# A transformer-like block: the second piece's product with v in float16 parts, earlier weight conversions, and products of ones on TensorE

## The chip, the core and the metric

One core of a Trainium2 chip runs the whole program. The metric is device time in microseconds of that core, as the median of several runs. TensorE multiplies matrices into PSUM; VectorE (DVE), ScalarE (ACT) and GpSimd (POOL) work on the results; SyncE (SP) issues nearly all transfers.

## What is computed

Attention over 2 batches, 8 heads, 768 positions and a head size of 64, with a window of 128 keys and 4 sink keys; then a layer norm and a two-layer channel network (512 to 2048 to 512) with a residual; then a gate by sine and cosine, a mixing over positions and a last channel product.

```python
scores = scale * np.matmul(q, k.transpose(0, 1, 3, 2))
scores = np.where(is_sink | in_window, scores, -1e9)
a = softmax(scores);  x = np.matmul(a, v)              # attention
xn = (x - mu) / np.sqrt(var + 1e-06) * g_ln
x = x + np.maximum(xn @ w_ch1, 0.0) @ w_ch2            # channel network
theta = x @ w_theta
y = einsum(w_tok_r, x * cos(theta)) + einsum(w_tok_i, x * sin(theta))
u = x + y
out = u + np.maximum(u @ w_ch, 0.0)
```

## The kernel before

The 1536 rows are cut into six pieces of two tiles of 128 rows. For each piece the attention runs head by head (`attn_fast`, a generator whose steps are drawn by the main loop): scores `s` (line 273), then the masked maximum on VectorE (394) and the exponential on ScalarE (397) into `p`. The channel network runs in 56 units `u`; a piece takes part in 16 of them (piece 0 in units 0 to 15, piece 1 in 8 to 23, and so on). In unit u, `first(u+1)` (649 or 670) computes one block of hidden values `h` and `second(u)` (696) adds its product to `acc`. The steps of the attention of the next piece are put between these parts by `advance`, so that TensorE's order is written out by hand; the queues of the other engines are ordered by a scheduler that goes by its own estimate of times. Each engine works its queue strictly in order.

Pieces 0 and 1 (`TURNED = 2`) turn their weights on TensorE: `turn_w` transposes `p` into a bank `wp` (443), and one engine, ScalarE for even heads (449) and VectorE for odd ones (447), copies it to `wt` in float32. One head later, `values` multiplies `wt` by `v` in float32 (477); each float32 product is two instructions in the trace. Sinks have their own small transpose (457), copy (458) and product. The result, divided by the sums, goes to `x` (494). For these pieces v is loaded whole (`whole_v`, 203). Pieces 2 to 5 split weights and v into a large and a small float16 part (`send_w`, `split_v` with lines 196 and 198), turn them by a transposing transfer (430), and need three float16 products for each float32 one.

Weights of the channel network come as 64-bit words. `load_w12(f)` reads two of 512 KB into raw buffers, of which there are four, and converts each with VectorE (555), ScalarE (556 and 558) and VectorE again (559). Four loads (`PRE`) are placed in piece 0's attention; later ones stand in the loop over units, held behind `relu` of that unit (`behind`). `AHEAD = (2, 3)` says that up to f = u + 2 is loaded in unit u, and up to u + 3 from unit 7 on. Units 0 to 7 use the weights in float32; from f = 8 they are split into two float32r parts first (637, 638).

The banks for `wp` are `ab[1:]` (three) during piece 0 and one, `a3`, later; `pv` has one bank during piece 1. `range_v` and `range_whole` find the largest v for a check at the end; `range_whole` loads tiles of v that were never split once more.

Of the kernel before, what the change touches and what calls it, by code (L numbers as in the profile page):

```python
# [8 lines left out]
F32 = mybir.dt.float32  # L9
F32R = mybir.dt.float32r  # L10
F16 = mybir.dt.float16
# [38 lines left out]
READY2 = 13.0  # L50
RATE = 7.0
PRE = [10, 15, 20, 24]
AHEAD = (2, 3)
START = 2
EARLY = 38.0

# [13 lines left out]
class Net:  # L70
# [110 lines left out]
    def split_v(self, b, t):  # L181

        if (b, t) in self.v3:
            return
        nc, p = self.nc, self.att
        r = p["vr"].tile([128, DM], F32, tag="vr", name="vr")
        nc.sync.dma_start(out=r, in_=self.vt[b, t])
        if t == NT:
            o = p["v"].tile([128, DM], F16, tag="vk", name="vk", bufs=1)
            nc.scalar.activation(o, r, AF.Copy, scale=VSC)  # L190
            r, lo, hi = r[64:96], o[64:96], o[64:96]
            self.v3[b, t] = o
        else:
            o = p["v"].tile([128, 2, DM], F16, tag="v", name="v")
            hi, lo = o[:, 0], o[:, 1]
            nc.scalar.activation(hi, r, AF.Copy, scale=VSC)
            self.v3[b, t] = hi, lo
        nc.vector.scalar_tensor_tensor(out=lo, in0=r, scalar=VSC, in1=hi, op0=ALU.mult, op1=ALU.subtract)
# [76 lines left out]
    def attn_fast(self, eng):  # L275

        steps = [(piece, h) for piece in range(NP) for h in range(H)]
        nc, p, qk, scored, turned, sent, late = self.nc, self.att, {}, [], [], [], []

        def load(j, eng=eng):  # L280
            if j < len(steps):
                piece, h = steps[j]
                if h % 2 == 0:
                    qk[piece, h] = qk[piece, h + 1] = self.split_qk(piece, h // 2, eng)

        def load_v(piece):
            if piece < NP:
                b, tiles = self.tiles(piece)
                if piece < TURNED:
                    for t in tiles:  # L290
                        self.whole_v(b, t)
                    return
                for t in ([tiles[0] - 1] if tiles[0] else []) + tiles + ([NT] if tiles[-1] >= 2 else []):
                    self.split_v(b, t)

        def ahead(piece):
            return self.tc.high_priority() if piece < TURNED else ExitStack()

        def turn():

            piece, h, pt, st = scored.pop(0)
            b, tiles = self.tiles(piece)
            with ahead(piece):
                blocks = self.turn_w(pt, tiles, h)
            sinks = []
            if tiles[0]:
                p["ws"].append(p["ws"].pop(0))
                sinks = [p["ws"][-1][0:NSK, i] for i in range(PIECE)]
                if not turned:

                    pool, tag = self.vbanks[self.vturn % len(self.vbanks)]
                    self.vturn += 1
                    with ahead(piece):
                        self.turn_sinks(pool.tile([128, 512], F32, tag=tag, name="pv"), pt, sinks)
            turned.append((piece, h, blocks, sinks, st, pt))

        def finish(head):

            piece, h, blocks, sinks, st = head[:5]
            b, tiles = self.tiles(piece)  # L320
            with ahead(piece):
                self.values(b, h, tiles, piece, blocks, sinks, st, turned[0] if turned and turned[0][3] else None)
                if h % (H // 2) == H // 2 - 1:
                    self.stats(piece, h // (H // 2))
            if h == V_RANGE:
                while late:
                    q, ts = self.tiles(late.pop())
                    for t in ts:
                        if (q, t) in self.v3:
                            with self.behind():  # L330
                                self.range_v(q, t)
            if h == H - 1:
                with ahead(piece):
                    self.norm(piece)
                late.append(piece)

        load(0, self.nc.vector)
        load_v(0)
        for j, (piece, h) in enumerate(steps):
            b, tiles = self.tiles(piece)  # L340
            if h == 0:
                self.x[piece] = self.xp.tile([128, PIECE, DM], F32, tag=f"x{piece}", name=f"x{piece}")
            load(j + 2)
            if h == (3 if piece else V_NEXT) and piece != TURNED - 1:
                load_v(piece + 1)
            pt, st = yield from self.softmax(h, tiles, qk[piece, h])
            if piece < TURNED:
                scored.append((piece, h, pt, st))
            else:
                sent.append((piece, h) + self.send_w(pt, tiles) + (st,))  # L350
            if piece < TURNED and h == H - 1:

                while scored:
                    turn()
                    yield
                    finish(turned.pop(0))
                    yield
                while turned:
                    finish(turned.pop(0))
                if piece == TURNED - 1:  # L360
                    load_v(piece + 1)
                yield
                continue
            if len(scored) > (TURN if piece < TURNED else 0):
                turn()
                yield

            if len(turned) > (1 if scored else 0):
                finish(turned.pop(0))
            elif len(sent) > LAG:  # L370
                finish(sent.pop(0))
        while sent:
            yield
            finish(sent.pop(0))
        for t in tiles:
            self.range_v(b, t)
        self.range_whole()

    def softmax(self, h, tiles, qk):

        nc, p = self.nc, self.att
        n = len(tiles)
# [2 lines left out]
        for i, t in enumerate(tiles):  # L385
# [10 lines left out]
                op1=ALU.min, accum_out=st[:, 0, i:i + 1]),  # L396
                nc.scalar.activation(e, e, AF.Exp, bias=st[:, 0, i:i + 1], scale=-1.0,  # L397
                                     accum_out=st[:, 1, i:i + 1])]
        self.inverse(st, PSC * VSC if qk[1] is not None else 1.0)
        return pt, st  # L400

    def send_w(self, pt, tiles):
# [30 lines left out]
    def turn_w(self, pt, tiles, h):  # L433

        nc = self.nc
        pool, tag = self.wbanks[self.wturn % len(self.wbanks)]
        self.wturn += 1
        ps = pool.tile([128, 512], F32, tag=tag, name="wp")
        keys = [(i, t - 1 + c) for i, t in enumerate(tiles) for c in range(2) if t + c]
        m = len(keys)  # L440
        for x, (i, t) in enumerate(keys):
            c0 = (t + 1 - tiles[i]) * KW
            nc.tensor.transpose(ps[:, x * 128:(x + 1) * 128], pt[:, i, c0:c0 + 128], self.ident)  # L443
        wt = self.att["wt"].tile([128, m, 128], F32, tag="wt", name="wt")
        ps = ps[:, 0:m * 128].rearrange("p (m k) -> p m k", k=128)
        if h % 2:
            nc.vector.tensor_copy(wt, ps)
        else:
            nc.scalar.activation(wt, ps, AF.Copy)
        return {(i, 0, t): wt[:, x] for x, (i, t) in enumerate(keys)}  # L450

    def turn_sinks(self, bank, pt, sinks):

        nc = self.nc
        ps = bank[0:NSK, 256:512].rearrange("p (i k) -> p i k", k=128)
        for i in range(PIECE):
            nc.tensor.transpose(ps[:, i], pt[:, i, 128:128 + NSK], self.ident)
        nc.vector.tensor_copy(self.att["ws"][-1][0:NSK], ps)

    def values(self, b, h, tiles, piece, blocks, sinks, st, after):  # L460

# [3 lines left out]
        pv = pool.tile([128, 512], F32, tag=tag, name="pv")  # L465
        hc = slice(h * D, (h + 1) * D)
        for i in range(len(tiles)):
            if piece < TURNED:
                prods = [(a, self.whole[b, t][:, hc]) for (j, e, t), a in blocks.items() if j == i]
                if sinks:  # L470
                    prods.append((sinks[i], self.whole[b, 0][0:NSK, hc]))
            else:
                prods = [(a, v[:, hc]) for (j, e, t), a in blocks.items() if j == i for v in self.v3[b, t][:2 - e]]
                if sinks:
                    prods.append((sinks[i], self.v3[b, NT][:, hc]))
            for j, (a, m) in enumerate(prods):
                nc.tensor.matmul(pv[:, i * D:(i + 1) * D], a, m, start=j == 0, stop=j == len(prods) - 1)  # L477
# [342 lines left out]
    def run(self, general):  # L820
# [27 lines left out]
        else:  # L848
# [2 lines left out]
            a["wbuf"] = [w.tile([128, 5 * PIECE, 128], F16, name=f"w{i}") for i in range(3)]  # L851
            for w in a["wbuf"]:
                nc.gpsimd.memset(w[:, 0:PIECE], 0.0)
            ws = rp("a_ws")
            a["ws"] = [ws.tile([128, PIECE, 128], F32, name=f"ws{i}") for i in range(2)]
            raw = rp("a_raw")
            attn = self.attn_fast
        self.rawp = [(self.xp, f"x{NP - 2 + i}") for i in range(2)] + ([] if general else [(raw, f"r{i}") for i in range(2)])
# [3 lines left out]
        pe = tc.manual_schedule(engines={mybir.EngineType.PE})  # L862
        pe.__enter__()
        side = attn(nc.vector)
        self.sbanks, self.vbanks, self.wbanks = [sb, hb, hb], [vb, ab[0]], ab[1:]
        self.tbanks = [hb, hb]
        n = 0
        while 0 not in self.xnorm:
            next(side)
            n += 1  # L870
            if n == 1:
                self.late()
            if n in PRE and not general:
# [225 lines left out]
```

## Time and profile before

| What | Value |
|---|---|
| runs | 617.91, 623.66, 625.28 us (median 623.66) |
| profiled execution | 617.65 us, of which the profile's span is 615.9 |
| busy, share of the span | TensorE 95%, VectorE 66%, ScalarE 54%, GpSimd 10% |
| mean granted TensorE clock | 0.983 |

All rows are of the one profiled execution, with times from the start of the span. TensorE's matrix products and its loading of weights are separate rows (PE and PEld). The end of a product is modelled, and products overlap, so that the time from one start to the next says more than the duration of one. Names such as `pv<-v,wt` are output and inputs; L477 is line 477. The granted clock is 1.00 at 2.4 GHz and half that at 1.2. In a row by stretch stand: start and end, length, then for PE, PEld, DVE, ACT and POOL the busy time with the number of instructions, the granted clock, the busy share of the transfer engines, and GB/s.

### The profile page before, as it was taken

To read this page: it belongs to the slowest core of one execution; us is meant where nothing else is said; L and a number is where in the kernel's file an instruction comes from. 1 tells how busy PE (TensorE), PEld (TensorE's weight loads), DVE (VectorE), ACT (ScalarE), POOL (GpSimd) and SP (SyncE) were. 2 spreads that over 40 slices of the span, in tenths; PEclk is the share of its full clock that TensorE was granted. 3 is DMA by queue.
4 is the path that set the end of the run, shared out by engine and by line. 5 is a ranking of instruction groups with operands and counts; after the bars stand their busy time and mean duration, and the time that the engine had idled before them with its cause. 6 is when DMAs were issued, how large, how long until landed. Compare 5 with 4: busy or idle time off the path is not lost.

```text
span 615.9 us, 9332 instructions
## 1 busy us (share of the span) xinstructions
PE 584.7 (95%) x3473; PEld 479.8 (78%) x3473; DVE 408.5 (66%) x925; ACT 334.0 (54%) x732; POOL 60.1 (10%) x53
## 2 busy tenths in 40 slices
PE   5969998899999999999999899999999899999996
PEld 3756666577777777777788678888999789999996
DVE  4763465889867776976775643367798789754262
ACT  3834563998755656655556633346676656532020
POOL 1000000000000000000021200001343332300100
PEclk9999997899999999999999989999999999999998
DMA  7641442789722533433312310000232322010112
GB/s 274 215 159 44 160 156 86 251 209 222 130 54 49 117 82 71 96 69 60 78 54 101 103 51 2 0 1 1 102 104 104 103 69 70 1 35 34 36 36 74
DMA packets 55367, 56.41 MB, mean 92 GB/s; under 512 B 40080, under 2 KB 43152, under 8 KB 55312
## 3 DMA queue, kind: packets, MB, share of 16 engines
q1 hardware_dynamic: 55312, 55.72, 32.0%
q8 instruction: 29, 0.48, 0.3%
q14 instruction: 26, 0.21, 0.1%
HBM read 43.12 MB, written 3.15 MB: 75 GB/s over the span
## 4 chain that ended last, share of the span: by engine, by line
PE 69%; DVE 13%; DMA 7%; ACT 6%; issue 2%; POOL 1%; SPq 0%; ACTq 0%; POOLq 0%
PE acc L696 19%; PE h L670 18%; PE s L273 9%; PE m L781 5%; PE f L812 5%; PE pv L477 5%; PE h L649 3%; DVE st L559 2%; DMA raw<-wtok 2%; DMA raw<-w 2%; PE th L740 2%; PE wp L443 2%; ACT st L558 1%; ACT raw L556 1%; DVE st L555 1%
## 5 line engine op out<-in xcount | busy, mean ns | idle before, releaser
L638 DVE TENSOR_TENSOR wl<-w,wh 128x512 fp32r<-128x512 f32 x96 | 69.0, 723 | 53.4 <-ACT wh L637 26.7
L637 ACT ACTIVATE wh<-w 128x512 fp32r<-128x512 f32 x96 | 59.9, 628 | 77.5 <-PE acc L696 44.0
L670 PE MATMUL h<-xT,wh 128*128 128x512 f32 (+1 forms) x384 | 96.8, 388 | 2.4 <-DVE w L555 2.4
L670 PEld LDWEIGHTS h<-xT,wh 128*128 128x128 f32 x384 | 67.1, 191 | 18.2 <-ACT xT L625 2.6
L696 PE MATMUL acc<-wh,hh 128*128 128x512 f32 x176 | 73.2, 416 | 0.0
L397 ACT ACTIVATE p<-p,st 128x272 f32<-128x272 f32 (+1 forms) x96 | 47.4, 494 | 43.7 <-DVE st L394 43.3
L696 PE MATMUL acc<-wl,hh 128*128 128x512 f32 x176 | 69.6, 395 | 0.0
L696 PE MATMUL acc<-wh,hl 128*128 128x512 f32 x176 | 69.5, 395 | 0.0
L394 DVE CUSTOM_DVE_ANT_0 p<-s,mask 128x272 f32<-128x272 f32 (+1 forms) x96 | 39.3, 411 | 29.7 <-PE s L273 28.9
L670 PE MATMUL h<-xT,wl 128*128 128x512 f32 (+1 forms) x192 | 48.8, 376 | 0.0
L696 PEld LDWEIGHTS acc<-wh,hh 128*128 128x128 f32 x176 | 33.5, 190 | 9.4 <-issue 1.2
L556 ACT ACTIVATE raw<-raw 128x512 f32<-128x512 f32 (+1 forms) x52 | 37.0, 715 | 6.5 <-DVE st L555 6.4
L670 PEld LDWEIGHTS h<-xT,wl 128*128 128x128 f32 x192 | 35.0, 191 | 6.8
L477 PE MATMUL pv<-v,wt 128*128 128x64 f16 (+1 forms) x472 | 38.2, 228 | 1.9 <-DVE x L494 1.9
L696 PEld LDWEIGHTS acc<-wh,hl 128*128 128x128 f32 x176 | 33.5, 190 | 7.8 <-DVE hl L675 0.3
L696 PEld LDWEIGHTS acc<-wl,hh 128*128 128x128 f32 x176 | 33.4, 190 | 6.0 <-DVE wl L638 0.4
L767 POOL TENSOR_TENSOR x<-xh,xl 128x512 f32<-128x512 f32 x12 | 19.3, 1607 | 131.1 <-DVE r L761 131.1
L597 POOL TENSOR_TENSOR rs<-rs,mhalf 128x2 f32<-128x2 f32 x6 | 4.8, 805 | 266.9 <-ACT rs L596 266.9
L675 DVE SCALAR_TENSOR_TENSOR hl<-h,hh 128x512 fp32r<-128x512 f32 (+1 forms) x48 | 30.7, 639 | 0.2 <-ACT hh L674 0.2
L273 PE MATMUL s<-raw 64*128 64x272 f32 (+1 forms) x64 | 24.1, 520 | 6.9 <-DMA raw<-qk 6.4
L558 ACT ACTIVATE st<-raw 128x768 uint16<-128x768 uint16 (+1 forms) x20 | 19.4, 971 | 18.6 <-DMA raw<-wtok 7.2
L674 ACT ACTIVATE hh<-h 128x512 fp32r<-128x512 f32 (+1 forms) x48 | 26.5, 552 | 5.5 <-PE h L670 5.5
(287 smaller groups left out, 1442.3 us busy)
## 6 DMA issues: line engine op xcount, KB each, us to landing
raw<-w SPq DMA_DIRECT2D x32, 512.0 KB, 4.3
raw<-wtok SPq DMA_DIRECT2D x12, 768.0 KB, 4.2
raw<-qk SPq DMA_DIRECT2D x16, 336.0 KB, 3.0
vr<-vt SPq DMA_DIRECT2D x14, 256.0 KB, 3.0
out_dram<-o SPq DMA_DIRECT2D x24, 128.0 KB, 1.7
raw<-qk SPq DMA_DIRECT2D x8, 272.0 KB, 4.0
raw<-wth SPq DMA_DIRECT2D x4, 512.0 KB, 3.3
raw<-wch SPq DMA_DIRECT2D x4, 512.0 KB, 3.3
```

Of the source, the lines that this page charges most:

```text
L273: self.nc.tensor.matmul(ps, q[:, c], k[:, k0:k0 + kn], start=j == 0, stop=j == len(prods) - 1)
L394: self.newest = [nc.vector.tensor_tensor_reduce(out=e, in0=ps[:, c0:WIN], in1=self.mask[min(t, 2)], scale=-0.125, scalar=3e38, op0=ALU.add ...
L397: nc.scalar.activation(e, e, AF.Exp, bias=st[:, 0, i:i + 1], scale=-1.0, accum_out=st[:, 1, i:i + 1])]
L477: nc.tensor.matmul(pv[:, i * D:(i + 1) * D], a, m, start=j == 0, stop=j == len(prods) - 1)
L556: nc.scalar.activation(hi.bitcast(F32), hi.bitcast(F32), AF.Copy, scale=2.0 ** -112)
L637: nc.scalar.activation(hi, r, AF.Copy)
L638: nc.vector.tensor_tensor(out=lo, in0=r, in1=hi.bitcast(F32), op=ALU.subtract)
L670: nc.tensor.matmul(ps[:, 0:n], a[:, k * 128:(k + 1) * 128], x[:, k, c], start=m == 0, stop=m == 11)
L675: nc.vector.scalar_tensor_tensor(out=hl, in0=ps[:, 0:n], scalar=0.0, in1=hh.bitcast(F32), op0=ALU.max, op1=ALU.subtract)
L696: nc.tensor.matmul(ps, a[:, c], w, start=m == 0 and n == 0, stop=m == NF - 1 and n == len(prods) - 1)
L781: nc.tensor.matmul(ps, z[i][e][:, c * 128:(c + 1) * 128], w[:, t], start=s == 0 and m == 0 and c % 2 == 0, stop=s == NT - 1 and m == 5 and ...
L812: nc.tensor.matmul(ps, self.w_last[k][e][:, c * 128:(c + 1) * 128], u[k][f], start=m == 0, stop=m == 11)
```

## The change

Five things change. Piece 1 takes v and weights in float16 parts: `turn_w` and `turn_sinks` write a large part with ScalarE and a small part with VectorE for every head, and `values` makes three float16 products where it made one of float32. Its v is split (tiles 1, 2, 3 and the sinks' tile, with a new small part `vl` of the sinks) instead of loaded whole; the v of piece 2 is asked for at head 3 of piece 1 and no longer at its end. `AHEAD` becomes (4, 4). At the very start 13 products of ones are put on TensorE, and one more behind every step that is drawn until piece 0 is normalized, 27 in all. Their operand is set once by VectorE, and bank `a3` is theirs during piece 0, so that `wp` has two.

```diff
-AHEAD = (2, 3)
+AHEAD = (4, 4)
+STIR = (13, 1)
...
             nc.scalar.activation(o, r, AF.Copy, scale=VSC)
+            if b == 0:
+                self.vl = p["v"].tile([128, DM], F16, tag="vl", name="vl", bufs=1)
+                nc.vector.scalar_tensor_tensor(out=self.vl[0:32], in0=r[0:32], scalar=VSC, in1=o[0:32], op0=ALU.mult,
+                                               op1=ALU.subtract)
...
-                if piece < TURNED:
+                if piece == 0:
                     for t in tiles:
                         self.whole_v(b, t)
...
-                blocks = self.turn_w(pt, tiles, h)
+                blocks = self.turn_w(pt, tiles, h if piece == 0 else None)
...
-                sinks = [p["ws"][-1][0:NSK, i] for i in range(PIECE)]
+                sinks = [[p["ws"][-1][0:NSK, e, i] for e in range(2)] for i in range(PIECE)]
...
-            if h == (3 if piece else V_NEXT) and piece != TURNED - 1:
+            if h == (3 if piece else V_NEXT):
                 load_v(piece + 1)
...
-                if piece == TURNED - 1:
-                    load_v(piece + 1)
...
+    def stir(self, n):
+        for _ in range(n):
+            self.nc.tensor.matmul(self.spoon, self.ones[:, 0:128], self.ones, start=True, stop=True)
...
+        if h is None:
+            wt = self.att["wt"].tile([128, 2 * m, 128], F16, tag="wt", name="wt")
+            nc.scalar.activation(wt[:, 0:m], ps, AF.Copy, scale=PSC)
+            nc.vector.scalar_tensor_tensor(out=wt[:, m:], in0=ps, scalar=PSC, in1=wt[:, 0:m], op0=ALU.mult,
+                                           op1=ALU.subtract)
+            return {(i, e, t): wt[:, e * m + x] for e in range(2) for x, (i, t) in enumerate(keys)}
...
-        nc.vector.tensor_copy(self.att["ws"][-1][0:NSK], ps)
+        ws = self.att["ws"][-1]
+        nc.scalar.activation(ws[0:NSK, 0], ps, AF.Copy, scale=PSC)
+        nc.vector.scalar_tensor_tensor(out=ws[0:NSK, 1], in0=ps, scalar=PSC, in1=ws[0:NSK, 0], op0=ALU.mult,
+                                       op1=ALU.subtract)
...
-            if piece < TURNED:
+            if piece == 0:
                 prods = [(a, self.whole[b, t][:, hc]) for (j, e, t), a in blocks.items() if j == i]
-                if sinks:
-                    prods.append((sinks[i], self.whole[b, 0][0:NSK, hc]))
             else:
                 prods = [(a, v[:, hc]) for (j, e, t), a in blocks.items() if j == i for v in self.v3[b, t][:2 - e]]
-                if sinks:
+                if sinks and piece < TURNED:
+                    prods += [(sinks[i][e], v[0:NSK, hc]) for e, v in (
+                        (0, self.v3[b, NT]), (0, self.vl), (1, self.v3[b, NT]))]
+                elif sinks:
                     prods.append((sinks[i], self.v3[b, NT][:, hc]))
...
+            self.ones = a["wbuf"][2][:, PIECE:PIECE + 4]
+            nc.vector.memset(self.ones, 1.0)
+            self.ones = self.ones.rearrange("p m k -> p (m k)")
...
-        self.sbanks, self.vbanks, self.wbanks = [sb, hb, hb], [vb, ab[0]], ab[1:]
+        self.sbanks, self.vbanks, self.wbanks = [sb, hb, hb], [vb, ab[0]], ab[1:] if general else ab[1:3]
+        if not general:
+            self.spoon = self.ps_a.tile([128, 512], F32, tag="a3", name="spoon")
+            self.stir(STIR[0])
...
         while 0 not in self.xnorm:
             next(side)
             n += 1
+            if not general:
+                self.stir(STIR[1])
```

## Rows read from the trace of the kernel before

**Rows 1.** Busy time by stretch (start:end, length, each engine's busy us, clock, DMA).

```profile
8.57:32.40 23.83, 23.81 (x84) 17.96 (x84) 16.60 (x63) 18.21 (x57) 0.00 (x0) 1.00 0.74 265
...
50.30:89.00 38.70, 38.70 (x190) 26.66 (x190) 20.26 (x64) 23.17 (x60) 0.00 (x0) 1.00 0.41 135
89.00:105.00 16.00, 13.27 (x48) 9.15 (x46) 7.98 (x20) 3.60 (x9) 0.83 (x1) 0.79 0.24 83
105.00:125.00 20.00, 17.61 (x66) 11.60 (x66) 17.93 (x47) 20.00 (x50) 0.00 (x0) 0.83 0.70 218
```

**Rows 2.** Chain of work, 5 to 35 us: start, us, what, count.

```profile
6.42 1.76 PE s L273 x6
...
14.33 1.63 PE s L273 x4
15.96 0.83 PE wp L443 x3
16.79 1.17 PE pv L477 x6
17.96 1.63 PE s L273 x4
```

**Rows 3.** Order of time, 30 to 58 us, TensorE: start, us, what.

```profile
32.93 2.66 PE L477 MATMUL pv<-v,wt 128*128 128x64 f32 x12
...
35.52 2.18 PE L273 MATMUL s<-raw 64*128 64x272 f32 x4
...
50.29 1.18 PE L273 MATMUL s<-raw 64*128 64x272 f32 x4
```

**Rows 4.** Chain of work, 50 to 365 us.

```profile
51.47 0.59 PE wp L443 x4
...
57.47 1.70 PE pv L477 x12
...
96.40 3.24 PE pv L477 x12
99.64 3.71 PE h L649 x8
...
106.09 1.92 PE h L649 x8
...
120.57 3.57 PE h L670 x8
...
126.41 2.04 PE h L670 x8
...
361.63 3.40 PE h L670 x15
```

**Rows 5.** What TensorE waited for, 36 to 165 us: total, times, longest.

```profile
PE h L670 <- DVE w L555: 2.4, 1, 2.4
PE pv L477 <- DVE x L494: 1.9, 1, 1.9
```

**Rows 6.** Groups, 50 to 95 us: busy us, mean ns | idle before.

```profile
L558 ACT ACTIVATE w<-raw 128x512 uint16<-128x512 uint16 x8 | 6.2, 770 | 0.0
...
L559 DVE SCALAR_TENSOR_TENSOR w<-raw,w 128x512 int32<-128x512 int32 x8 | 5.3, 677 | 0.5 <-ACT w L558 0.5
L556 ACT ACTIVATE raw<-raw 128x512 f32<-128x512 f32 x8 | 5.2, 656 | 0.0
...
L555 DVE TENSOR_SCALAR w<-raw 128x512 uint16<-128x512 uint16 x7 | 3.2, 456 | 7.3 <-DMA raw<-w 7.3
...
L458 DVE COPY ws<-pv 16x256 f32<-16x256 f32 x7 | 2.9, 411 | 6.9 <-PE pv L457 6.8
...
L449 ACT ACTIVATE wt<-wp 128x512 f32<-128x512 f32 x4 | 2.4, 588 | 2.1 <-PE wp L443 2.1
```

**Rows 7.** Groups, 9.7 to 33 us.

```profile
L196 ACT ACTIVATE v<-vr 128x512 f16<-128x512 f32 x1 | 0.6, 612 | 0.0
```

**Rows 8.** Line 477 alone by stretch: a head of piece 2.

```profile
128.20:129.50 1.30, 0.58 (x14) 0.46 (x14) 1.00 0.86 318
```

More of the change, by code (lines that the diff above doesn't have):

```diff
@@ L343, in attn_fast @@
             load(j + 2)
-            if h == (3 if piece else V_NEXT) and piece != TURNED - 1:
+            if h == (3 if piece else V_NEXT):
                 load_v(piece + 1)
-            pt, st = yield from self.softmax(h, tiles, qk[piece, h])
+            pt, st = yield from self.softmax(b, h, tiles, qk[piece, h])
             if piece < TURNED:
@@ L377, in attn_fast, with softmax @@
         self.range_whole()
-    def softmax(self, h, tiles, qk):
+    def stir(self, n):
+        for _ in range(n):
+            self.nc.tensor.matmul(self.spoon, self.ones[:, 0:128], self.ones, start=True, stop=True)
+    def softmax(self, b, h, tiles, qk):
         nc, p = self.nc, self.att
@@ L398, in softmax @@
                                      accum_out=st[:, 1, i:i + 1])]
-        self.inverse(st, PSC * VSC if qk[1] is not None else 1.0)
+        self.inverse(st, PSC * VSC if tiles[0] or b else 1.0)
         return pt, st
@@ L443, in turn_w @@
             nc.tensor.transpose(ps[:, x * 128:(x + 1) * 128], pt[:, i, c0:c0 + 128], self.ident)
+        ps = ps[:, 0:m * 128].rearrange("p (m k) -> p m k", k=128)
+        if h is None:
[4 more added lines that the diff above has]
+            return {(i, e, t): wt[:, e * m + x] for e in range(2) for x, (i, t) in enumerate(keys)}
         wt = self.att["wt"].tile([128, m, 128], F32, tag="wt", name="wt")
-        ps = ps[:, 0:m * 128].rearrange("p (m k) -> p m k", k=128)
         if h % 2:
@@ L853, in run @@
                 nc.gpsimd.memset(w[:, 0:PIECE], 0.0)
+            self.ones = a["wbuf"][2][:, PIECE:PIECE + 4]
+            nc.vector.memset(self.ones, 1.0)
+            self.ones = self.ones.rearrange("p m k -> p (m k)")
             ws = rp("a_ws")
-            a["ws"] = [ws.tile([128, PIECE, 128], F32, name=f"ws{i}") for i in range(2)]
+            a["ws"] = [ws.tile([128, 2, PIECE, 128], F16, name=f"ws{i}") for i in range(2)]
             raw = rp("a_raw")
```

## Prediction

> **What bounds the kernel now.** Read the busy time by stretch first, because a share over the whole span hides stages with different limits [rows 1]. From 8.57 to 32.40 us (attention of piece 0) TensorE is busy all the time, ScalarE 18.21 of 23.83 us, VectorE 16.60. From 50.30 to 89.00 (units 0 to 5 with piece 1's attention) TensorE is again full, the others at 23.17 and 20.26 of 38.70. From 89 to 125 TensorE loses 5.1 us (16.00 - 13.27 and 20.00 - 17.61), and the granted clock is 0.79 and 0.83.
>
> Then read the chain of work, where the first stretch is one pattern per head, six times over: s, wp, pv, 3.63 us from 14.33 to 17.96 [rows 2]. So TensorE's own work sets this stretch. Its speed there is the surprise: the clock column says 1.00, but durations say otherwise. The same four score products take 2.18 us at 35.52 and 1.18 us at 50.29 [rows 3]; twelve pv instructions take 2.66 us at 32.93 and 1.70 at 57.47 [rows 3, 4]. Piece 0's attention runs at the lower of the two levels (1.2 GHz), although TensorE is never idle; the 1.00 stands there because no change of level was recorded before. A level is read from the duration of one form.
>
> Last the waits. Between 36 and 165 us TensorE waits 1.9 us for VectorE's x and 2.4 us for its w [rows 5]. Both times VectorE is itself held: its first step of a weight conversion (L555) stands in the queue and waits for the transfer, 7.3 us in all between 50 and 95 [rows 6]. After both waits TensorE runs at half speed for a while: eight h products take 3.71 instead of 1.92 us, eight others 3.57 instead of 2.04 [rows 4].
>
> **Stirring, piece 0.** Added are 13 products of 128x512 ahead of the first score and one behind each of the 27 steps of piece 0, three per head. A one-pass product of 512 columns takes 3.40 / 15 = 0.227 us at the full level [rows 4] and 3.57 / 8 = 0.446 at the lower [rows 4].
> The 13 take 3.0 to 5.8 us. TensorE has nothing to do before 6.42 us [rows 2]; if the ones are set by 2 us, the delay of the first score is 0 to 1.4 us. I take 0.5. If the setting of the ones stands on VectorE behind the wait for the small inputs it would be more, up to 5.8 us; the scheduler is free to put it before that wait, so I don't expect it.
> At the full level a head costs: s 1.63 x 1.18 / 2.18 = 0.88; wp 0.59 x 3 / 4 = 0.44; pv 1.70 x 6 / 12 = 0.85; three stirs 0.68; together 2.85 instead of 3.63 [rows 2 to 4]. Six periods give 4.7 us and the last twelve pv instructions 0.9 (2.66 - 1.70): bound 5.6 us. ScalarE allows less: its 18.21 us grow by three conversions of v of 0.612 [rows 7] to 20.05, which leaves 3.8 us of 23.83. Some conversions of weights there may slip behind the stretch, so the value lies between: -4.5 us. At the lower level the 27 stirs cost 27 x 0.446 = +12.0 us instead. Why I expect the full level: with units between the heads the same s, wp and pv run at it from 50 to 89 us, so a mix in which long products stand between them is enough there [rows 1, 4]; and stirs are such products.
> Bank a3 goes to the stirs and two banks are left to wp: zero, since a bank is wanted again two heads on and its eviction takes 0.588 us at most [rows 6]; uncovered it would be that.
>
> **pv of piece 1 in float16 parts.** Per head 12 instructions (1.70 us [rows 4]) go, and 18 float16 products come. Fourteen such products take 0.58 us in piece 2 [rows 8], 41 ns each: 18 x 0.041 = 0.75. Saved per head 0.95 us; seven heads at full level 6.6 us, and the eighth, which runs at half speed behind the first wait, 3.24 - 2 x 0.75 = 1.7 us [rows 4].
> What it adds lies on the other engines. Each head's weights are now read by ScalarE (0.588) and by VectorE (0.677, the nearest 128x512 operation of that kind), where before one of them did it, four heads each; the sinks need a ScalarE copy more (bound by VectorE's 0.411); tiles 1 and 2 of v are converted too, which falls into piece 0 and is counted above [rows 6, 7]. Between a wp and its pv lie 6.0 us (51.47 to 57.47 [rows 4]), which hide the second eviction; uncovered, 0.7 us per head. The sinks' lower part and the x behind it now wait for ScalarE; x is wanted one head later, when the single pv bank comes round.
> Is there room? With conversions four units ahead, two loads more fall between 50 and 89: ScalarE 4 x (0.770 + 0.656) = 5.7 us, VectorE 4 x (0.677 + 0.456) = 4.5 us. ScalarE then has 23.17 + 4 x 0.588 + 7 x 0.411 + 5.7 = 34.1 us; VectorE 20.26 + 4 x 0.677 + 4.5 and its 7.3 us of waiting for transfers = 34.8 of 38.70 [rows 1, 6]. So of the 6.6 us VectorE lets 3.9 through: -3.9 (bounds 0 and -6.6), and -1.7 for the eighth head.
>
> **Conversions four units ahead.** The load of f is held behind relu of unit f-4, where it was behind f-2 and, from unit 7 on, f-3 with two loads in that unit. The hold binds ScalarE's conversions; L555 and the transfers run as early as the four raw buffers allow, before and after. So one load per unit stays, and with it a VectorE that waits in its queue. What goes is the bunch: units 6 and 7 convert f = 8, 9 and 10 just where TensorE needs f = 8, ScalarE is full there (20.00 of 20.00 [rows 1]), and the second wait stands there. I let that wait go whole: 2.4 us, and the half speed behind it: twelve products, eight of which cost 3.57 - 2.04 = 1.53, so 2.3. Together -4.7. The first wait (1.9, and 3.71 - 1.92 = 1.8 behind it [rows 4, 5]) I let stand: nothing moves the load that VectorE waits for off that queue. Bounds: 0 and -8.4.
> The later load of v for piece 2 and the two fewer loads for the range of v lie beside full TensorE stretches: 0.
>
> **Sum.** 0.5 - 4.5 - 3.9 - 1.7 - 4.7 = -14.3. The profiled execution took 617.65 us (span 615.9): 603.4. The runs shown are 617.91, 623.66 and 625.28; with the profiled one their mean is 621.1, 3.5 above the profiled. I add that and forecast 606.5, some 2.7% under the median.
>
> **Rivals.**
> First, the other engines take over in piece 1: VectorE waits for transfers as before, the faster pv only lengthens TensorE's waits, and the second wait turns up elsewhere. For it: 34.8 of 38.70 us are spoken for, and a hold that doesn't bind L555 may change nothing. Against it: before, only two of those waits reached TensorE. Left is 0.5 - 4.5 - 1.7 = -5.7: 612, or 615.5 on the runs' scale. This is also the case that the conversions ahead don't do what they say. 0.22.
> Second, everything comes: -5.6 - 6.6 - 1.7 - 8.4 = -22.3: 595.4, runs 599. 0.13.
> Third, slower: the stirs don't lift the level in piece 0. In a 3.63 us period at the lower level s, wp and pv leave no gap, and yet it didn't rise in 24 us, so that being busy alone isn't it [rows 1, 2]. Then the price is 12.0 + 1.4 in the first 35 us; with the rest as forecast (-10.3) that is 617.65 + 3.1 = 620.8, runs 624. It decides against the change from the point where the stirs stay low and the rest brings under 1 us: then 630. 0.14.
> On this the Trainium skill, "TensorE: Matmul & The Clock Gate", section "A second HAM failure mode: psum-queue depth-cycling", tells of a kernel whose TensorE idles briefly between groups of products and so falls back and forth between the levels. By that rule the stirs would not hold the level and the third rival's time results; the trace bears it out behind the waits of 1.9 and 2.4 us [rows 5], and not from 50 to 89 us, where the level holds [rows 1].
>
> **Chances.** Forecast 0.50 (its own range 600 to 613), rivals 0.22, 0.13, 0.14. A measurement of this kernel can tell about 2% from no change: faster means under 611 against the median, slower over 636 (or over 630 against the profiled execution). Faster: most of the forecast (0.42) and the second rival, 0.55. Slower: half of the third rival, 0.07. Same: the rest, 0.38. Range 595 to 622: it leaves out the best of the second rival and the upper part of the third.
>
> **What would show it.** Step one is right if the period of s in piece 0 falls to about 3 us and s takes about 1.2 us for four; wrong if it rises to 5.0. Step two: pv groups of some 0.75 us; the stretch to the end of piece 1's heads shorter by about 4 us beyond that; wrong if TensorE shows new waits for VectorE's x or ws, or for a lower part of wt. Step three: no wait of h L670 for VectorE's w at the first h of unit 8, and no half-speed products there. The forecast fails most easily by a VectorE that waits for transfers at other places than now.

## The result and the profile after

| | before | after |
|---|---|---|
| median of the runs | 620.39 us (616.71 to 625.99, 20 runs) | 627.14 us (623.40 to 633.67, 20 runs) |
| profiled execution | 617.65 us, span 615.9 | 633.67 us, span 631.9 |
| mean granted clock | 0.983 | 0.943 |

The ratio is 1.0102 [1.0077, 1.0126]: the changed kernel is 1% slower, where 2.7% faster was forecast. The profiled execution of after is the longest of its 20 runs; the low clock is in all of them (0.943 to 0.959), so that its times are read for what happens, and the sizes come from the medians. The medians differ by 6.75 us, the two traces by 16.0.

Busy time by stretch of after, with the columns of [rows 1]:

```profile
10.00:13.00 3.00, 1.38 (x6) 0.61 (x7) 1.79 (x8) 2.27 (x10) 0.00 (x0) 1.00 1.03 419
13.00:16.00 3.00, 3.00 (x9) 1.50 (x9) 0.82 (x5) 1.56 (x8) 0.00 (x0) 0.53 0.84 328
16.00:47.00 31.00, 31.00 (x102) 21.32 (x100) 16.47 (x55) 18.23 (x50) 0.00 (x0) 0.50 0.43 145
...
100.00:115.00 15.00, 10.01 (x58) 6.24 (x56) 9.47 (x22) 6.91 (x17) 0.00 (x0) 0.68 0.35 108
```

TensorE is idle for 1.62 of the 3 us from 10 to 13. Then the granted clock falls from full (2.4 GHz) to one half (1.2 GHz) and stays there for over 30 us, although TensorE is busy all the time. The chain of work shows what a head then costs (start, us, what, count; `spoon` is a product of ones):

```profile
17.82 0.72 PE s L279 x2
18.55 0.54 PE spoon L386
19.09 1.20 PE s L279 x2
20.29 0.54 PE spoon L386
20.83 0.64 PE wp L452 x3
21.47 0.43 PE spoon L386
21.90 1.17 PE pv L496 x6
23.07 0.72 PE s L279 x2
```

From s to s it is 5.25 us, where before it was 3.63 [rows 2]; the three products of ones take 1.51 of it. Behind the attention of piece 0 comes the first transpose of the normalized piece, in the chains of work of before and after:

```profile
41.78 1.98 PE tp L615 x8
56.01 1.98 PE tp L634 x8
```

That is 14.2 us later. From there to the first product of the gate (432.74, before 416.91) it is 376.7 us, before 375.1: the loss lies in piece 0. These 376.7 us also hide a gain: in the changed kernel without stirs (below) the same way is 370.3 us. This longest execution has a wait of 2.3 us for the maxima of the scores, ending at 151 us, with the half level for some 10 us behind it, which the trace of before does not have.

What emptied TensorE is seen in the order of time, 9 to 13 us (start, us, engine, line, output and input, and in brackets the idle time before and what ended it):

```profile
9.81 0.63 ACT L202 ACTIVATE v<-vr 128x512 f16<-128x512 f32 x1 [7.60 <-DMA vr<-vt]
...
10.35 0.39 ACT L406 ACTIVATE p<-p,st 128x128 f32<-128x128 f32 x1
10.47 0.69 DVE L204 SCALAR_TENSOR_TENSOR v<-vr,v 128x512 f16<-128x512 f32 x1 [1.99 <-ACT v L202]
...
10.97 0.30 PE L452 MATMUL wp<-ident,p 128*128 128x128 f32 x1 [0.66 <-ACT p L406]
11.08 0.43 DVE L403 CUSTOM_DVE_ANT_0 p<-s,mask 128x272 f32<-128x272 f32 x1
...
11.56 0.52 ACT L406 ACTIVATE p<-p,st 128x272 f32<-128x272 f32 x1 [0.73 <-DVE st L403]
...
12.23 0.44 PE L452 MATMUL wp<-ident,p 128*128 128x128 f32 x2 [0.96 <-ACT p L406]
```

The split of the first v of piece 1 (a conversion into a large float16 part by ScalarE, and the difference as a small part by VectorE) was put by the scheduler ahead of the first softmax. ScalarE's half (line 202) starts after 7.60 idle us, when its transfer has landed; only then comes the first exponential. VectorE's half (204) waits for ScalarE's, and behind it stands the second masked maximum (403), and behind that the second exponential. TensorE, which wants the weights of the first head, waits 0.66 and 0.96 us.

These are TensorE's three longest waits from 36 to 165 us, first for the norm of piece 0 (total, times, longest):

```profile
PE tp L634 <- DVE xn L621: 6.8, 1, 6.8
PE wp L452 <- DVE wt L457: 4.3, 2, 3.8
PE s L279 <- DVE st L403: 3.2, 3, 2.3
```

Before, the wait for the norm was the longest too; [rows 5] leave it out:

```profile
PE tp L615 <- DVE xn L602: 4.1, 1, 4.1
```

Both waits of [rows 5] have changed: h for w is gone, and pv for x is 1.7. In piece 1 a new one stands for the small part of `wt` (457), which only the changed kernel has. Its chain:

```profile
82.69 0.83 PE pv L496 x18
...
95.21 3.83 DMA raw<-qk
99.05 0.76 ACT hi L252
100.09 0.56 ACT raw L575
100.65 0.66 ACT w L577
101.31 0.52 ACT raw L575
101.83 0.66 ACT w L577
102.48 0.46 ACT p L406 x2
102.94 0.49 ACT wt L456
103.46 0.70 DVE wt L457
...
112.16 3.62 PE h L668 x8
```

The float16 product itself came as costed: 0.83 us for 18 instead of 1.70 for 12 [rows 4]. But ScalarE stands in its queue behind a split of q and k that waits for its transfer, then behind four weight conversions (2.4 us); the weights of the last heads come late, and eight h products take 3.62 us once more, as in [rows 4].

### The profile page after: what moved, and what is told of

Its sections match the earlier page's. It is cut to its first block, busy times and chain, and to the rows that moved or that the text cites. A ratio compares the mean times of both kernels' runs of the same rounds, so it can differ in the third digit from the quotient of the medians.

```text
span 631.9 us, 9540 instructions
## 1 busy us (share of the span) xinstructions
PE 597.0 (94%) x3561; PEld 479.5 (76%) x3561; DVE 413.0 (65%) x931; ACT 339.6 (54%) x746; POOL 60.2 (10%) x53
## 4 chain that ended last, share of the span: by engine, by line
PE 63%; DVE 14%; ACT 9%; DMA 8%; issue 3%; POOL 1%; SPq 0%; ACTq 0%; DVEq 0%; POOLq 0%
PE acc L715 18%; PE h L689 17%; PE s L279 7%; PE m L800 5%; PE f L831 5%; PE pv L496 4%; DMA raw<-w 3%; DMA raw<-wtok 2%; DVE st L578 2%; ACT raw L575 2%; PE th L759 2%; PE h L668 2%; PE spoon L386 2%; ACT st L577 1%; DVE st L574 1%
## 5 line engine op out<-in xcount | busy, mean ns | idle before, releaser
L496 PE MATMUL pv<-v,wt 128*128 128x64 f16 (+1 forms) x504 | 33.4, 214 | 1.7 <-DVE x L513 1.7
L578 DVE SCALAR_TENSOR_TENSOR w<-raw,w 128x512 int32<-128x512 int32 x32 | 21.6, 687 | 11.5 <-ACT w L577 11.3
```

Of the source, the lines that this page charges most:

```text
L578: nc.vector.scalar_tensor_tensor(out=dst, in0=hi, scalar=3, in1=dst, op0=ALU.logical_shift_left, op1=ALU.bitwise_or)
```

## Experiments

All ratios are to the kernel before, timed on the same chip; the brackets are 95% intervals. A stir is a product of ones, and a step one of the 27 of piece 0. The kernel with three stirs per step has a single run and stands in its own part below.

| kernel | median us | ratio [95%] |
|---|---|---|
| after | 627.14 | 1.0102 [1.0077, 1.0126] |
| before + stirs | 617.44 | 0.9935 [0.9912, 0.9958] |
| before + float16 pv | 618.41 | 0.9952 [0.9927, 0.9976] |
| before + conversions ahead | 614.23 | 0.9899 [0.9867, 0.9931] |
| before + stirs and conversions ahead | 613.08 | 0.9899 [0.9875, 0.9924] |
| after without stirs | 613.77 | 0.9888 [0.9834, 0.9941] |
| after, split of v later | 612.79 | 0.9872 [0.9817, 0.9928] |
| the same, two stirs per step | 611.13 | 0.9881 [0.9852, 0.9909] |

**Without stirs.** Piece 1 and the conversions stay.

```diff
-STIR = (13, 1)
+STIR = (0, 0)
```

> The changed kernel without any product of ones (bank a3 stays reserved). Theory: the 27 products behind the steps run at the lower level, 0.43 us each, so that piece 0's attention gets some 11 us shorter: 616 us, where the changed kernel has 627 and the kernel before 620. Rival: the loss stands behind piece 0, in waits of VectorE and TensorE; then the time stays above 623. The period of a head in piece 0 should return to 3.6 us in both.

It took 613.77 us, and a head of piece 0 3.63 us, as before. By the ratios the stirs cost the changed kernel 2.1%, some 13.3 us (1.0102 against 0.9888, of 620.39). They don't cost it alone, though: without them the scheduler also puts the split of v elsewhere, behind the first exponentials:

```profile
8.48 0.40 ACT L406 ACTIVATE p<-p,st 128x128 f32<-128x128 f32 x1 [6.26 <-DVE st L403]
11.18 0.62 ACT L202 ACTIVATE v<-vr 128x512 f16<-128x512 f32 x1
```

It is the same in the float16 product alone (8.61 and 11.32 us), which has no stirs either, while with one or three stirs per step the split stands ahead (9.81). So the 13.3 us are the price of the stirs together with the place of the split that came with them. Why the scheduler's estimate moves with the stirs, no run shows.

**Stirs alone.** The kernel before with the products of ones, and a3 kept for them.

> The kernel before with the products of ones alone (13 and one behind each step, bank a3 reserved, ones set by VectorE). Theory: in the changed kernel the level fell at 13 us because ScalarE waits for the transfer of v (vr) before its first exponentials, so that TensorE stands idle near 11 us. Without the split of v there is no such wait, the level holds, a head takes about 3 us instead of 3.63, and the time is 616 us. Rival: the mix of scores, transposes, pv and one product of ones does not hold the level whatever happens at 11 us; then a head takes about 5 us and the time is 631 us.

It is faster, 0.9935. Its chain of work in piece 0:

```profile
16.30 0.61 PE pv L483 x6
16.91 0.48 PE s L274 x2
17.40 0.32 PE spoon L383
17.72 0.65 PE s L274 x2
18.37 0.32 PE spoon L383
18.69 0.37 PE wp L449 x3
19.06 0.22 PE spoon L383
19.28 0.61 PE pv L483 x6
```

A head takes 2.98 us from pv to pv here (2.87 for the next): s, wp and pv run at the full level (2.4 GHz), with one product of 512 columns behind each step. The 13 products at the start had brought the level up by the first scores (two of them take 0.65 us at 7.95 us, as at 17.72), and this mix then holds it. The first transpose comes at 39.72 instead of 41.78, though, and not 4 us sooner: VectorE waits for raw weights in its queue ahead of the norm, and TensorE 6.5 us for the norm (4.1 before).

**The split of v later.** One number: the v of piece 1 is asked for at head 5 of piece 0, behind the first softmaxes.

```diff
-V_NEXT = 2
+V_NEXT = 5
```

> The changed kernel with the split of v for piece 1 asked for at head 5 of piece 0 instead of head 2. Theory: ScalarE's first exponentials no longer stand behind the conversion that waits for v, TensorE has no gap near 11 us, the level holds through piece 0 and the time falls by up to 11.6 + 4.5 us, to 611 us. Rival (the mix does not hold the level): 627 us, a period of 5.2 us as before. A third way: the scheduler puts the conversion in the same place; then nothing moves.

612.79 us, 2.3% under after by the ratios. From 10 to 16 us TensorE is never idle and the level holds. The price comes later: ScalarE waits 2.26 us for the transfer of the third split (26.01 us), and behind it stand four conversions of weights and the exponential that TensorE wants next; TensorE waits 1.72 us for it, until 30.88 us, and the clock falls behind that (0.60 in 30 to 34, 0.50 in 34 to 40).

**A conversion on ScalarE alone ahead of the first exponentials.** Stirs alone, with one more tile of v that ScalarE converts and that nobody reads.

```diff
+            if j == 0:
+                extra = p["vr"].tile([128, DM], F32, tag="vr", name="vr")
+                nc.sync.dma_start(out=extra, in_=self.vt[0, 2])
+                half = p["v"].tile([128, DM], F16, tag="vx", name="vx", bufs=1)
+                nc.scalar.activation(half, extra, AF.Copy, scale=VSC)
```

> e2_stir_only with one thing more: a tile of v is loaded at the start and converted by ScalarE, ahead of its first exponentials, as in the changed kernel; nobody reads it. Theory: ScalarE waits for that transfer until about 9.8 us, TensorE is idle near 11 us, the level falls and stays low through piece 0, a head takes about 5.2 us, and the time is 10 to 13 us above e2_stir_only (617.4): 629. Rival: the level falls in the changed kernel for another reason; then only the delay of some 1.5 us at the start shows, 619 us, with a head at 2.9 us.

A miss: 618.86 us, 0.9985 [0.9959, 1.0010], and the level held. The conversion ran from 9.14 to 9.77 us, VectorE's maxima went ahead of it, and TensorE waited only 0.4 us. Against stirs alone (0.9935 [0.9912, 0.9958]) it costs 0.5%, with intervals that just miss each other, but not the level. So ScalarE's half is not enough.

**The same with VectorE's half.** Before the first maximum VectorE now takes the difference, as after does.

```diff
+                nc.vector.scalar_tensor_tensor(out=half, in0=extra, scalar=VSC, in1=half, op0=ALU.mult,
+                                               op1=ALU.subtract)
```

> e6_stir_gap, where TensorE waited only 0.4 us and the level held, with the second half of the conversion too: VectorE makes the small part and stands in its queue ahead of the first maximum, as it stands ahead of the second in the changed kernel. Nobody reads the result. Theory: TensorE now waits some 1.5 us near 11 us, the level falls and stays low through piece 0, a head takes about 5.2 us and the time is 10 us or more above e2_stir_only (617.4): 628. Rival: the level falls in the changed kernel for another reason, and only the delay shows: 620, with a head below 3 us.

634.87 us, 1.0236 [1.0199, 1.0273]: 3.0% over stirs alone, from one tile of v that is 0.63 us on ScalarE and 0.69 on VectorE. TensorE's wait, 9 to 14 us, and its stretches:

```profile
PE s L274 <- DVE st L407: 1.8, 1, 1.8
```

```profile
10.00:13.00 3.00, 2.22 (x7) 1.08 (x7) 1.90 (x10) 2.09 (x9) 0.00 (x0) 0.68 1.04 417
...
16.00:30.00 14.00, 14.00 (x46) 9.57 (x45) 7.24 (x26) 8.69 (x23) 0.00 (x0) 0.50 0.40 140
```

This is the changed kernel's loss, made in a kernel that holds nothing else of its piece 1. It shows the cause: a split at the head of both queues. With it come the wait of 1.8 us and then the low level until the attention of piece 0 is over (a head takes 5.25 us, the first transpose comes at 54.17).

**Three stirs per step.** After, with

```diff
-STIR = (13, 1)
+STIR = (13, 3)
```

> The changed kernel with three products of ones behind each step instead of one, nine a head; the wait for v near 11 us stays. Theory A: with that many long products the level comes back after the wait; a head then takes about 2.2 + 9 x 0.23 = 4.2 us, and the run is some 7 us below the changed kernel: 620. Theory B: it stays low whatever is added between; a head takes 3.63 + 9 x 0.43 = 7.5 us, and the run is at 645.

614.85 us, a single run. The split of v stands at the same place (line 202 at 9.81 us) and the transpose that waited starts at the same 12.23 us. But TensorE has more to do until then, and its stretches are

```profile
10.00:13.00 3.00, 2.48 (x12) 1.11 (x11) 1.77 (x8) 2.04 (x9) 0.00 (x0) 1.00 1.03 419
13.00:16.00 3.00, 3.00 (x15) 1.42 (x14) 0.81 (x5) 2.08 (x7) 0.00 (x0) 1.00 0.86 335
```

0.52 us are idle instead of 1.62, and the level holds through the attention of piece 0. In this run the filled gap did no harm; it doesn't show whether three stirs would lift a level that has fallen. Two more stirs per step are not free: a head takes 4.16 us.

**Split later and two stirs.**

> e3_v_late with two products of ones behind each step instead of one. In e3_v_late the level fell at about 31 us, behind a wait of 1.7 us. Theory: six products a head hold it through the end of piece 0; they cost 27 x 0.23 = 6 us of TensorE's time, of which most lies in its waits, and the products of the last two heads get 2 us faster: 611. Rival: TensorE has no waits left to hide them, 616.

611.13 us, 0.9881 [0.9852, 0.9909], the lowest median of all, though by its ratio it can't be told from the split later alone or from conversions ahead alone. The clock stays at 1.00 up to 34 us, yet the first transpose comes at 43.17, since it waits 5.3 us for the norm.

**The float16 product alone.**

> The kernel before with the float16 parts of piece 1 alone (no products of ones, conversions ahead as before, three banks for wp). Theory by the sum of the prediction: 3.9 + 1.7 us less than before, 615 us. Rival: VectorE and ScalarE, now with two evictions a head, hold TensorE, and the time is that of before or up to 5 us more.

618.41 us, 0.9952: 3.0 us. TensorE's longest wait from 30 to 165 us, and the stretch from 115 to 125:

```profile
PE wp L452 <- DVE wt L457: 4.9, 1, 4.9
```

```profile
115.00:125.00 10.00, 8.51 (x22) 5.52 (x22) 8.52 (x22) 10.00 (x30) 0.00 (x0) 0.66 0.90 240
```

The new wait for `wt` is there without stirs and without conversions ahead, and the clock of 0.66 at 115 to 125 stands as in the kernel before.

**Conversions ahead alone.**

```diff
-AHEAD = (2, 3)
+AHEAD = (4, 4)
```

> The kernel before with the conversions four units ahead alone. Theory by the sum of the prediction and by the step from e4_pv_only to e1_no_stir (618.4 to 613.8): the second wait goes, 4 to 5 us less than before, 617 us. Rival: conversions ahead help only where pv is in float16 parts, and alone the time is that of before (622).

614.23 us, 0.9899: 6.3 us. Of TensorE's five waits from 30 to 165 us the last:

```profile
PE pv L477 <- DVE x L494: 0.8, 1, 0.8
```

The first is 4.3 us for the norm, the three between are 0.9, 0.9 and 0.8 us. h for w is gone (0.9 us for VectorE's `xT` is left there) and pv for x has fallen from 1.9 to 0.8 [rows 5]; from 115 to 125 us the clock is 1.00. This one line is worth nearly all that any version reached. Float16 pv on top of it (after without stirs, 0.9888) adds 0.1%, which the intervals can't tell from nothing.

**Stirs and conversions ahead.**

> The kernel before with the conversions four units ahead and with the products of ones, pv in float32 as before. Theory: without the split of v nothing falls, the two gains (6.3 of e5_ahead_only and 4.6 of e2_stir_only) lie in different stretches and add: 610. Rival: what the stirs gain in piece 0 is lost again to the loads that VectorE waits for, which come no earlier: 614.

613.08 us, 0.9899: not the sum of the two. The first transpose comes at 39.51 us, 2.4 before conversions ahead alone (41.95), but it has waited 6.5 us for the norm, and the stretch of 95 to 105 is at 0.66 in both.

**Two banks for the turned weights.** In the kernel with the split later, piece 1's scores give up one of their two banks to `wp`.

```diff
-        self.sbanks, self.vbanks, self.wbanks = [sb, ab[2]], [vb], [ab[3]]
+        self.sbanks, self.vbanks, self.wbanks = [sb], [vb], ab[2:]
```

> e3_v_late with two banks for wp during piece 1 (a2 and a3) and one for its scores instead of two. Theory: the wait of TensorE for the second eviction of wt near 88 us (4.0 us) and the lower level behind it come from the single bank of wp; they go, and the time falls by 4 to 6 us to 607. Rival: the weights are not ready anyway, and the wait moves on to pv or to the scores, which now have one bank; then 612 to 616.

622.44 us, 1.0044 [1.0016, 1.0073], slower than the split later alone (0.9872). The wait for `wt` goes, and s waits for the maxima, eight times and 10.6 us in all.

**VectorE writes both parts of the weights.** Again in the kernel with the split later.

```diff
-            nc.scalar.activation(wt[:, 0:m], ps, AF.Copy, scale=PSC)
+            nc.vector.tensor_scalar(out=wt[:, 0:m], in0=ps, scalar1=PSC, scalar2=None, op0=ALU.mult)
```

> e3_v_late with both parts of wt in piece 1 written by VectorE, so that the eviction of wp no longer stands behind ScalarE's conversion of q and k and of weights. Theory: the wait of TensorE for wt near 88 us (4.0 us) and the half speed behind it come from ScalarE's queue; they go, and the time falls by 4 to 6 us to 608. Rival: VectorE has no room for 8 x 0.6 us more (and waits for transfers itself); then the wait stays or moves, 612 to 616.

612.51 us, 0.9894 [0.9878, 0.9911], not told from the split later alone. In the profiled execution, the longest of its five (618.54 us), TensorE no longer waits for `wt`, but 4.0 us for the exponentials (line 406) and 3.6 for x.

**The load of q and k later.** Split later with two stirs, and the first load of q and k for piece 2 behind the last softmax of piece 1.

> The kernel of this run is that of v_late_two (split of v for piece 1 after the softmaxes of its first units, stirs 13 and 2; 611.1 us) with the first load and split of q and k for piece 2 asked for after the last softmax of piece 1 instead of at its seventh head. Theory (ScalarE stands behind the split of q and k, which waits for its transfer, and so wt of the last heads comes late): the wait of TensorE for wt on VectorE near 88 to 92 us (3.9 us at its longest) goes, the clock does not fall behind it, and the time comes to about 607 us. Rival (the wait only moves): the first scores of piece 2 wait for q and k by as much, and the time stays at 610 to 612 us.

612.01 us, 0.9877 [0.9813, 0.9940]: no gain. The edit missed its target. It moved the first of two splits, which doesn't wait (78.71 to 79.72 us). The second stood at 86.35 us behind a wait of 2.72 for its transfer, as it had at 85.45 behind 2.83, and TensorE's wait for `wt` was 3.7 us, as before.

**The norm first.** In the kernel with the split later and two stirs, VectorE's steps of the weight conversions are held behind the last step of the norm.

```diff
-                self.newest = [self.relu[u]]
+                self.newest = [self.relu[u], self.normed]
```

> The kernel of this run is that of v_late_two with VectorE's steps of the weight conversion held behind the last step of the norm. Theory (VectorE's conversions, waiting for their transfers of raw weights, stand ahead of the norm's steps at the end of piece 0): the first transposes come 2 to 4 us earlier than the 43.2 us of v_late_two, and the time comes to about 608 us. Rival (the norm waits on its own inputs, or the transposes' gain is lost at the next stall): the transposes move by under 1 us, or the time stays at 610 to 612 us.

The first transpose came 2.0 us earlier (41.16 instead of 43.17) and the wait for the norm fell from 5.3 to 3.7 us. The time did not: 613.71 us, 0.9891 [0.9826, 0.9955]. TensorE then waited longer for the maxima of the scores (3.0 us instead of 1.0) and, ahead of h, for x (2.2 instead of 0.9).

**Both.** The norm first and the load of q and k later, in one kernel.

> The kernel of this run has both edits of qk_late and norm_first. Theory: the two places are 45 us apart and add up, about 604 us, below every kernel so far. Rival: one of them gives nothing, 607 to 611 us.

613.22 us, 0.9879 [0.9816, 0.9943]. With one edit that missed and one that gained nothing, it tells no more.

**The split that waits, held back.** Split later with two stirs, and the second split of q and k issued behind the last large part of `wt`.

```diff
+        if (piece, pair) == (TURNED, 1):
+            with self.tc.issue_after(self.last_wt.ins):
+                nc.scalar.activation(hi, r, AF.Copy)
```

> The kernel of this run is that of v_late_two (611.1 us) with the split of the second pair of q and k for piece 2 on ScalarE, the one that waited 2.83 us for its transfer at 85.45 us there, held behind the last eviction of weights of piece 1. In qk_late the first pair was moved, which does not wait, and this split stood where it was. Theory (ScalarE's queue behind the split makes wt late): TensorE's wait for wt of 3.9 us falls to about 0.5, since 2.83 + 0.76 us go from ScalarE's queue ahead of it, and the time comes to about 607.5 us. Rival (the wait only moves, as it did in vector_hi and two_banks): the wait for wt falls, other waits of TensorE between 85 and 125 us grow by about as much, and the time stays at 610 to 612 us.

612.07 us, 0.9846 [0.9780, 0.9913], against 0.9881: the intervals overlap widely. The wait for `wt` at 84 to 96 us fell from 3.9 to 2.9 and not to 0.5. The chain of work in front of it:

```profile
85.75 0.39 ACT hh L674
...
88.97 0.49 ACT wt L460
...
89.48 0.70 DVE wt L461
```

With the split gone, ScalarE waits for h of the unit instead (2.6 us by the view of waits), and the same four conversions and two exponentials stand ahead of `wt` (86.14 to 88.97 us). The split was one of three things in that queue.

## Why the prediction failed

**The start: right.** First score 0.5 us later was forecast; it starts at 6.82 instead of 6.42 (7.14 with stirs alone).

**Stirs by themselves: right per head, the total in part by luck.** Forecast were 2.85 us per head and 4.0 us net; stirs alone gave 2.87 to 2.98 per head and 4.0 us (0.9935 of 620.39). But six heads at the full level gain some 4 us on TensorE, and the first transpose comes only 2.1 us earlier. The rest goes into the wait for the norm (6.5 us instead of 4.1), which neither [rows 5] nor the sum has; the prediction had ScalarE's room set the limit. In the traces only these 2.1 us are seen, and at the gate nothing is left of them (416.82 us, before 416.91); where the 4.0 us of the ratios arise is not shown.

**The tiles of v converted in piece 0: the step that failed.** The prediction counted them as busy time of ScalarE (three of 0.612 us), and they took 1.1 us off the bound of 5.6. It summed durations over a stretch and did not ask where in the queues they stand. With the stirs added, the first of them stands at the very front, ahead of the first softmax, and waits for its transfer there; VectorE's half, which the sum did not place at all, holds the second maximum. TensorE's 1.62 us of waiting are the small part of the price; the level that fell behind them is the large one, so that the stirs, forecast at -4.0 us, cost 13.3. Against stirs alone ScalarE's conversion costs 0.5%, ScalarE's and VectorE's together 3.0%: that was shown in a kernel without any other part. Neither part loses by itself: stirs alone gain 4.0 us, and without stirs the split stands behind the first exponentials. The sum had them as independent.

On this the Trainium skill, "PSUM — Partial Sum Buffer", section "Engine vs sequencer instructions", says that the queues of ScalarE, VectorE and GpSimd are strictly first in, first out. The rows at 9.81 to 11.56 us agree.

**The third rival: its price came, its mechanism by half.** It gave +12.0 + 1.4 = 13.4 us for stirs at the lower level; the stirs cost after 13.3 us, and the first transpose moved by 14.2. Its mechanism, that such a mix doesn't lift the level, holds once the level has fallen: in after and in the run with both halves of a split the mix didn't bring it back in over 30 us. It doesn't hold from the start: with stirs alone the level is up at the first scores and stays up for all of piece 0. The difference is one early wait. The prediction weighed the two levels by a chance of 0.14, and did not look for what could bring the level down, though it lay in the changed kernel's own queues.

For this rival the prediction named the Trainium skill, "TensorE: Matmul & The Clock Gate", section "A second HAM failure mode: psum-queue depth-cycling": in a kernel with short idle times between groups of products the level goes back and forth. What is seen here differs: with stirs alone the level holds through piece 0, and in piece 0 of after it fell once, behind the early wait, and stayed low from 13 us to behind 47, in a stretch without any idle time.

**pv in float16: the product right, the sum wrong.** 0.83 us per head against 1.70 is the 0.87 saved of the 0.95 forecast. The step that failed here is the second eviction of the weights, set at nothing because 6.0 us lie between a wp and its pv. At the end of piece 1 that cover is gone: ScalarE waits for a transfer or for h, converts weights, and TensorE waits 3.8 to 5.7 us for `wt` in each kernel that has this product on two engines and one bank. The prediction named this as a sign that would show it wrong ("a lower part of wt"), and its price for the uncovered case, 0.7 us per head, is the eviction alone, without what stands ahead of it. Of 5.6 us came 3.0 alone, and 0.1% on top of conversions ahead.

**Conversions ahead: right in kind, low in size.** Forecast 4.7 us, 6.3 measured alone. The second wait, for w, went whole, as forecast. The first, which was let stand, shrank from 1.9 to 0.8 us too.

**The sum** added parts as if they were independent. By the ratios the three parts alone give 4.0 + 3.0 + 6.3 = 13.3 us, close to the 14.3 forecast; the kernels that have all three and hold the level through the early gap give 1.1 to 1.5%, 6.6 to 9.5 us (two banks aside, which lost, and three stirs, a single run). That lies between the first rival (other engines take over, 5.7 us) and the forecast, nearer to the rival. From the forecast (-14.3) to the measurement (+6.3 by the ratio) it is 20.6 us: 17.3 of them lie in the stirs with the place of the split (-4.0 forecast, +13.3 measured) and 3.4 in the rest (-10.3 forecast, -6.9 by after without stirs). One slip of the working is small beside this: 603.4 and 3.5 make 606.9, not 606.5.

**What stays open.** Five edits to the waits at and behind the first transpose (two banks, VectorE's copy, the norm first, q and k later, the split held) took a wait away or shortened it, apart from q and k later, and none brought a gain beyond its interval. With two banks, VectorE's copy and the norm first the waits that grew in its place were seen, but no run shows one single cause. Whether ScalarE's four conversions between 86 and 89 us, moved out of that place, would give more, was not tried. Nor was a split ahead of the first softmax without stirs, or any mix that would bring a fallen level back in piece 0.

## What to carry to other kernels

An operation that is moved costs its place in each in-order queue, not only its duration: ask for every part of it what it waits for and what stands behind it, and if it may be placed ahead of the first work of a pipeline, hold it back by hand. An addition on one engine can also change the order that a scheduler gives to the others, so look at their queues again after each part. Filler products gained here at the full level only, so check the first gap behind which the level could fall, and whether the filler also fills that gap. Parts that each ease a different wait of one stretch don't add up when the engines behind them are nearly full; measure the smallest part alone first, since here one number gave nearly all of the gain.

## What was not expected of the hardware

- In piece 0 a wait of TensorE of 1.6 to 1.8 us (after; stirs with both halves; 1.72 in split later) was followed by the half level, and one of 0.4 to 0.5 us (ScalarE's half alone; three stirs per step) was not. The length of a wait doesn't decide it, though. Four transposes `wp` take 0.66 us behind a wait of 2.84 with the norm first (full level), and 1.19 behind a wait of 0.84 with conversions ahead alone (half level); what decides is not shown:

```profile
90.02 0.66 PE L452 MATMUL wp<-ident,p 128*128 128x128 f32 x4 [2.84 <-DVE wt L457]
90.56 1.19 PE L443 MATMUL wp<-ident,p 128*128 128x128 f32 x4 [0.84 <-ACT wt L449]
```

- Once it had fallen, the level stayed at 0.50 for 31 us with TensorE busy in 31.00 of 31.00 us (after); the same order of products held the full level when it had not fallen before (stirs alone, a head in 2.87 to 2.98 us instead of 5.25).
- In the kernel before the clock stands at 1.00 from 33 to 38 us while products run at half speed there [rows 3]; with stirs alone it says 1.00 from 16 to 30 us and products run at full speed. In both the level is read from durations, not from the column. The mean of 0.983 for the kernel before counts that stretch as full.
